# A fifth tile between the halves of the fourth, a one-tile unit's weight splits outside its branch, and a quarter of the descriptor memory

## The chip, the core and the metric

One core of a Trainium2 chip. The metric is the device time of one execution in microseconds. The core has five engines that run queues of instructions of their own and wait for each other by semaphores: TensorE (PE, matmuls and transposes; PEld is its weight loading), ScalarE (ACT), VectorE (DVE), GpSimd (Pool) and SyncE (SP, which here only issues transfers).

## The reference

An attention between tokens and a small state gives 4352 rows of 512 values (8 batches of 512 tokens and 32 state rows, eight heads side by side). Then a mixture of experts works on each row with one expert out of eight:

```python
logits = x @ w_gate
e_idx = np.argmax(logits, axis=1)
gate_w = probs[np.arange(N), e_idx]            # softmax of logits
eom = 1.0 / (1.0 + np.exp(-(x @ w_output_gate)))
for e in range(E):
    mask = e_idx == e
    h = np.maximum(x[mask] @ w1[e], 0.0)       # 512 -> 1024
    ye = h @ w2[e]                             # 1024 -> 512
    out[mask] = gate_w[mask, None] * eom[mask, e, None] * ye
```

## The kernel before

Until about 125 us the kernel does the attention and finds each row's expert. The rest, which the change touches, works through **units**: a unit is up to 512 rows of one expert, with a fifth tile of up to 128 more where the expert's last rows would otherwise need a unit of their own. The counts per expert are 1568, 632, 512, 541, 513, 40, 0 and 546, so nine units are executed, 0 to 8, of 14 in the program; the others lie behind branches. Units 0, 1 and 4 have four full tiles of 128 rows; 2, 3, 5, 6 and 8 have a fifth tile, which is narrow (64 rows or fewer) in four of them; unit 7 holds the 40 rows of expert 5, a single tile. A new expert begins at units 3 to 8.

All matmuls are made of three products: each operand is split into a high half (fp32r) and a low half, `xhi`, `xlo`, `whi`, `wlo`, `hhi`, `hlo`, and hi·hi, hi·lo and lo·hi are added in PSUM. For a unit:

- Pool gathers the unit's rows by indirect transfers, one for each tile (`fetch`, two units ahead), PE transposes them (`transposes`), ACT casts the high half and DVE subtracts for the low one (`x_halves`).
- `blocks` is the first layer, eight blocks f of 128 hidden columns, each with a relu (ACT) and a subtraction (DVE). Which columns stream through PE depends on the unit's class: `cls` 0 is the one-tile unit with a form of its own (rows as the stationary side, two matmul groups into `pbs`, relu into `hs`, eight transposes); 2 is four tiles, 3, 4 and 5 have a fifth.
- `tile_of(t)` is the second layer for a tile: `second` does 24 matmuls 128x512 into `po`, ACT scales the rows by `fac` into `y`, and Pool writes them out by an indirect transfer. `second_narrow` does a narrow fifth tile in 15 matmuls, with an evacuation of three steps (ACT, DVE, ACT).
- Where the next unit has another expert (`chgs`), its weights are split by `halves(i, h)`: for each of four stages i (0 and 1 the first layer's, 2 and 3 the second's) two halves h, each one ACT cast to `whi` and one DVE subtraction to `wlo`. SP loads the stages for a later expert with `load_behind` once they are split.

ACT, DVE, PE and Pool run in the order in which the code is written. Runtime classes are tested by branches on each engine; work in a branch that isn't taken is jumped over. `middle`, called in the middle of tile 0's 24 matmuls, holds splits and transposes for the next unit. Where a branch with transfers isn't taken, Pool executes an INC_SWDGE_SEM, which brings the semaphores of indirect transfers to the value that the others wait for.

Of the kernel before, what the change touches and what calls it, by code (L numbers as in the profile page):

```python
# [14 lines left out]
ALU = mybir.AluOpType  # L15
# [6 lines left out]
def attention_then_top1_experts(ctx: ExitStack, tc: tile.TileContext, x, state, w_gate, w_og, w1, w2, out):  # L22
# [113 lines left out]
    def unit_table():  # L136
# [64 lines left out]
        nc.vector.tensor_tensor(route_i[:, 4, 1:], uf[:, 0, 1:], uf[:, 0, :NU], op=ALU.is_gt)  # L201
        nc.vector.tensor_copy(units_i, cf[:, 5, E - 1 : E])

    tid_sb = const.tile([P, NQ], F32, name="tid_sb")
# [550 lines left out]

    def second(po, hhi, hlo, t, between=None):
        c = slice(P * t, P * t + P)
        for k in range(KH):
            if k == KH // 2 and between is not None:
                between()  # L760
            i, q = 2 + k // 4, k % 4
            nc.tensor.matmul(po, lhsT=hhi[:, k, c], rhs=whi[i][:, q, :], start=(k == 0), stop=False)  # L762
            nc.tensor.matmul(po, lhsT=hhi[:, k, c], rhs=wlo[i][:, q, :], start=False, stop=False)  # L763
            nc.tensor.matmul(po, lhsT=hlo[:, k, c], rhs=whi[i][:, q, :], start=False, stop=(k == KH - 1))  # L764

    def second_narrow(po):

# [30 lines left out]
        nc.scalar.copy(whi[i][:, c, :], stage[i][:, c, :])  # L798
        nc.vector.tensor_sub(wlo[i][:, c, :], stage[i][:, c, :], whi[i][:, c, :].bitcast(F32))  # L799

    def new_halves(i, h, chg):
        with tc.If(of(chg, ET.Activation, ET.DVE) == 1):
            halves(i, h)

    def load_behind(i, chg, s):

        nxt = value(3, s, [ET.SP], E - 1)
        nc.sync.dma_start(stage[i], (w1v if i < 2 else w2v)[bass.ds(nxt, 1), i % 2].rearrange("o p k f -> p (o k) f"),
                          cond=(of(chg, ET.SP) == 1), cond_hint=False)

    for i in (2, 3):
        stage[i] = bp1.tile([P, 4, 512], F32, name=f"stage{i}")
# [10 lines left out]
    hlo = bp1.tile([P, KH, UT * P], F32R, name="hlo")  # L823
    hs = bp1.tile([P, 2, 512], F32, name="hs")

    got, chgs, clss = {}, {}, {}
    table = unit_table()

    def second_stream(b, f, cls):
# [10 lines left out]
    def blocks_of_first_unit(cls, xg):  # L840
        evs = of(cls, ET.Activation, ET.DVE)
        cls = of(cls, ET.PE)
        for f in range(KH):
            if f == 0:
                first(pas[0], f, xhi, xlo, slice(0, NX))

                x_transposed(xg, 2, xhi, xlo)
                x_transposed(xg, 3, xhi, xlo)
            if f + 1 < KH:
                first(pas[(f + 1) % 2], f + 1, xhi, xlo, slice(0, NX))  # L850
            if f == 0:
                x_transposed(xg, 4, xhi, xlo)
            relu(hhi[:, f, :NX], hlo[:, f, :NX], pas[f % 2])
            next(table, None)
            b = pbs[f % 2]
            with tc.If(cls == 2) as c2:
                first(b[:, :256], f, xhi, xlo, slice(NX, NX + 256))
            with c2.Else():
                with tc.If(cls > 2):
                    second_stream(b, f, cls)  # L860
            with tc.If(evs > 2) as c3:
                relu_of_tail(f, b, evs)
            with c3.Else():
# [12 lines left out]
        chgs[1] = value(4, 1, [ET.Activation, ET.DVE, ET.SP], 1)  # L876
        for i in range(4):
            first_weights(i)
        return factors(0, xg)

    def blocks(s, cls, next_rows):

        cls = of(cls, ET.PE, ET.Activation, ET.DVE)
        nxt = chgs.get(s + 1)
        with tc.If(cls == 0) as c0:

            for i in range(2):
                for k in range(KX):
                    for x, w in ((xhi, whi), (xlo, whi), (xhi, wlo)):
                        nc.tensor.matmul(pbs[i], lhsT=x[:, k, :P], rhs=w[i][:, k, :], start=(k == 0 and w is whi and x is xhi),  # L890
                                         stop=(k == KX - 1 and w is wlo))
            new_halves(2, 0, chgs[s])
            new_halves(2, 1, chgs[s])
            nc.scalar.activation(hs[:, 0, :], pbs[0], AF.Relu)
            new_halves(3, 0, chgs[s])
            nc.scalar.activation(hs[:, 1, :], pbs[1], AF.Relu)
            for i, tp in enumerate((pos[1], pbs[0])):
                tp = tp.rearrange("p (q t) -> p q t", t=P)
                c = slice(4 * i, 4 * i + 4)
                for q in range(4):  # L900
                    nc.tensor.transpose(tp[:, q, :], hs[:, i, P * q : P * q + P], ident)
                if i == 0 and nxt is not None:
                    transposes(got[s + 1][1], 0)
# [28 lines left out]
        if nxt is not None:  # L932
            load_behind(0, nxt, s + 1)

    def step(s):
        idt, xg = got[s]
# [8 lines left out]
        if s == 0:  # L945
            fac = blocks_of_first_unit(cls, xg)
        else:
            if s + 2 < NU:
                got[s + 2] = fetch(s + 2)
            fac = factors(s, xg)  # L950
            if more:
                chgs[s + 1] = value(4, s + 1, [ET.Activation, ET.DVE, ET.SP], 1)
            blocks(s, cls, next_rows)
# [10 lines left out]
        def tile_of(t):  # L964
            po, y = pos[t % 2], ys[t % 3]

            def rows_of_tile():
                second(po, hhi, hlo, t, middle if more and t == 0 else None)
                if t == 0 and s and more:
                    next_rows(4)  # L970
# [15 lines left out]
            else:  # L986
                with tc.If(at == 5) as c5:  # L987
                    rows_of_tile()
                with c5.Else():
                    rows_of_narrow_tile()  # L990

        few = of(at, ET.PE, ET.Activation, ET.Pool)
        if s:
            tile_of(0)
            with tc.If(at > 0):
                tile_of(1)
                with tc.If(at > 1):
                    tile_of(2)
                    tile_of(3)
                    with tc.If(at > 2):  # L1000
                        tile_of(4)
        else:
            for t in range(UT):
                if t < 2:
                    for h in range(2):
                        new_halves(t, h, chgs[1])
                    load_behind(t, chgs[1], 1)
                if t == 0:
                    tile_of(0)
                else:  # L1010
                    with tc.If((few if t < UT - 1 else at) > (0, 0, 1, 1, 2)[t]):
                        tile_of(t)
                next_rows(*((), (0, 1), (2, 3), (4,), ())[t])

    with tc.manual_schedule(engines={ET.PE, ET.Activation, ET.DVE, ET.Pool}):
        got[0] = fetch(0)
# [12 lines left out]
        ids(nc.gpsimd, idx, hs[:, :, :NQ], tid_sb)  # L1029
        for s in range(SURE):  # L1030
            step(s)
        units = nc.values_load(units_i, engines=[ET.PE, ET.Activation, ET.DVE, ET.Pool, ET.SP], min_val=SURE, max_val=NU,
                               skip_runtime_bounds_check_because="a sum of rounded-up counts over the experts")
        with ExitStack() as ifs:  # L1034
            for s in range(SURE, NU):
                ifs.enter_context(tc.If(units > s))
                step(s)


# [22 lines left out]
```

## Time and profile before

| | us |
|---|---|
| median of 3 runs (581.37 to 582.8) | 582.47 |
| profiled execution, its own time | 583.2 |
| its span, first to last instruction | 581.1 |
| PE busy | 541.5 |
| DVE, ACT, Pool busy | 258.6, 237.7, 171.0 |

A span is one execution as the hardware profiler saw it. PE is the engine with the most work by far, so time is found where PE waits, and after its last matmul. The durations of single instructions are from this execution. PE's matmuls overlap: one of 128x512 is shown with 0.39 us, but the next begins 0.23 us behind it.

### The profile page before, as it was taken

How to read it: one execution, taken by the hardware profiler on the slowest of the kernel's cores; microseconds unless marked ns; L12 is line 12 of the kernel's file. 1: busy time of each engine (PE TensorE's matmuls, PEld its weight loads, DVE VectorE, ACT ScalarE, POOL GpSimd, SP SyncE). 2: the span in 40 equal slices, each digit the busy share in tenths (PEclk: the TensorE clock that was granted, in tenths of full speed). 3: DMA queues.
4: the chain of work that ended last, by engine and by line, in shares of the span. 5: the costliest groups of instructions: out<-in, count | busy, mean ns of one | idle time of the engine just before them, and what ended most of it. 6: DMA issues, size and time to landing. Idle time of an engine off the chain costs nothing. (4 is left out here: it accounts for less than half of the span.)

```text
span 581.1 us, 11555 instructions
## 1 busy us (share of the span) xinstructions
PE 541.5 (93%) x4028; PEld 462.5 (80%) x4028; DVE 258.6 (44%) x609; ACT 237.7 (41%) x400; POOL 171.0 (29%) x189
## 2 busy tenths in 40 slices
PE   7699989999999999999999999999999999599980
PEld 4578878659987888988998888889889987489860
DVE  3678788646712221360365046226506621755200
ACT  3767867533421221351353144235415423644210
POOL 5117778771534013101500240140024013240110
PEclk9999999999999999999999999999999999799995
DMA  9767524444763002232318133531813451852210
GB/s 252 205 216 234 159 82 147 132 129 150 263 251 118 18 22 83 69 96 105 108 32 295 55 116 103 211 108 50 301 56 105 137 192 48 294 188 76 109 58 12
DMA packets 45047, 78.23 MB, mean 135 GB/s; under 512 B 10312, under 2 KB 18504, under 8 KB 44936
## 3 DMA queue, kind: packets, MB, share of 16 engines
q1 hardware_dynamic: 37624, 52.49, 27.5%
q0 software_dynamic: 7312, 24.31, 12.7%
q8 instruction: 63, 1.03, 0.7%
q14 instruction: 48, 0.39, 0.2%
HBM read 68.38 MB, written 18.90 MB: 150 GB/s over the span
## 5 line engine op out<-in xcount | busy, mean ns | idle before, releaser
L762 PE MATMUL po<-whi,hhi 128*128 128x512 f32 x272 | 109.0, 401 | 4.7 <-ACT whi L798 4.7
L972 POOL DMA_INDIRECT out_dram<-y,idt x30 | 29.4, 981 | 279.4 <-ACT y L971 232.9
L764 PE MATMUL po<-whi,hlo 128*128 128x512 f32 x272 | 107.0, 393 | 0.0
L763 PE MATMUL po<-wlo,hhi 128*128 128x512 f32 x272 | 106.8, 393 | 0.0
L752 PE MATMUL pb<-xhi,whi 128*128 128x288 f32 (+4 forms) x256 | 83.2, 325 | 0.8 <-ACT y L971 0.8
L753 PE MATMUL pb<-xlo,whi 128*128 128x288 f32 (+4 forms) x256 | 83.1, 325 | 0.0
L754 PE MATMUL pb<-xhi,wlo 128*128 128x288 f32 (+4 forms) x256 | 83.1, 325 | 0.0
L971 ACT ACTIVATE y<-po,fac 128x512 f32<-128x512 f32 x34 | 23.5, 690 | 117.7 <-PE po L764 66.9
L799 DVE TENSOR_TENSOR wlo<-stage,whi 128x1024 fp32r<-128x1024 f32 x52 | 63.5, 1224 | 10.7 <-ACT whi L798 8.2
L714 POOL DMA_INDIRECT xg<-xa,idt x50 | 53.7, 1074 | 35.4 <-DVE idt L709 14.9
L762 PEld LDWEIGHTS po<-whi,hhi 128*128 128x128 f32 x272 | 51.6, 190 | 14.9 <-ACT whi L798 4.9
L764 PEld LDWEIGHTS po<-whi,hlo 128*128 128x128 f32 x272 | 51.5, 189 | 11.0
L763 PEld LDWEIGHTS po<-wlo,hhi 128*128 128x128 f32 x272 | 51.7, 190 | 10.1
L752 PE MATMUL pa<-xhi,whi 128*128 128x256 f32 x192 | 54.2, 282 | 3.5 <-ACTq L1000 2.1
L741 DVE TENSOR_TENSOR xlo<-pxT,xhi 128x512 fp32r<-128x512 f32 x50 | 32.7, 686 | 49.9 <-ACT xhi L740 38.3
L753 PE MATMUL pa<-xlo,whi 128*128 128x256 f32 x192 | 53.4, 278 | 1.1 <-issue 0.7
L798 ACT CAST whi<-stage 128x1024 fp32r<-128x1024 f32 x52 | 54.2, 1049 | 0.4 <-ACT ex L726 0.4
L754 PE MATMUL pa<-xhi,wlo 128*128 128x256 f32 x192 | 53.3, 278 | 0.0
L752 PEld LDWEIGHTS pb<-xhi,whi 128*128 128x128 f32 x256 | 48.1, 188 | 4.1 <-issue 1.3
L754 PEld LDWEIGHTS pb<-xhi,wlo 128*128 128x128 f32 x256 | 48.1, 188 | 2.9
L753 PEld LDWEIGHTS pb<-xlo,whi 128*128 128x128 f32 x256 | 48.1, 188 | 2.8
L740 ACT CAST xhi<-pxT 128x512 fp32r<-128x512 f32 x50 | 27.4, 589 | 38.8 <-PE pxT L736 38.2
(228 smaller groups left out, 860.8 us busy)
## 6 DMA issues: line engine op xcount, KB each, us to landing
stage<-in_moe_w_dram SPq DMA_DIRECT2D x42, 1024.0 KB
xa<-xm SPq DMA_DIRECT2D x7, 1056.0 KB
xb<-in_x_dram SPq DMA_DIRECT2D x7, 1024.0 KB
xb<-in_x_dram SPq DMA_DIRECT2D x4, 256.0 KB
xg<-xa,idt POOLq DMA_INDIRECT x50
out_dram<-y,idt POOLq DMA_INDIRECT x34
xa<-xm SPq DMA_DIRECT2D x1, 528.0 KB
sraw<-in_state_dram SPq DMA_DIRECT2D x1, 512.0 KB
```

Of the source, the lines that this page charges most:

```text
L714: nc.gpsimd.indirect_dma_start(out=xg[:, t, :], out_offset=None, in_=xa[:, :], in_offset=bass.IndirectOffsetOnAxis(ap=idt[:, t : t + 1], a ...
L740: nc.scalar.copy(xhi[:, :, c], pxTs[t % 2])
L741: nc.vector.tensor_sub(xlo[:, :, c], pxTs[t % 2], xhi[:, :, c].bitcast(F32))
L752: nc.tensor.matmul(ps, lhsT=hi, rhs=xhi[:, k, cols], start=(k == 0), stop=False)
L753: nc.tensor.matmul(ps, lhsT=hi, rhs=xlo[:, k, cols], start=False, stop=False)
L754: nc.tensor.matmul(ps, lhsT=lo, rhs=xhi[:, k, cols], start=False, stop=(k == KX - 1))
L762: nc.tensor.matmul(po, lhsT=hhi[:, k, c], rhs=whi[i][:, q, :], start=(k == 0), stop=False)
L763: nc.tensor.matmul(po, lhsT=hhi[:, k, c], rhs=wlo[i][:, q, :], start=False, stop=False)
L764: nc.tensor.matmul(po, lhsT=hlo[:, k, c], rhs=whi[i][:, q, :], start=False, stop=(k == KH - 1))
L798: nc.scalar.copy(whi[i][:, c, :], stage[i][:, c, :])
L799: nc.vector.tensor_sub(wlo[i][:, c, :], stage[i][:, c, :], whi[i][:, c, :].bitcast(F32))
L972: nc.gpsimd.indirect_dma_start(out=out[:, :], out_offset=bass.IndirectOffsetOnAxis(ap=idt[:, t : t + 1], axis=0), in_=y, in_offset=None)
```

## The change

1. **Tile 4** (`last_tile`) is called between the halves of tile 3's 24 matmuls instead of behind them. `second` does its products in pairs of k.
2. **The one-tile unit's splits.** Row 4 of `route_i`, which told whether the expert changes (1), tells 2 if the unit has at most 128 rows. In the branch `cls == 0` only the split of (2, 0) stays; (2, 1), (3, 0) and (3, 1) follow behind the branch, in an `If` of their own that other units pass by. The next unit's transposes and `x_halves` of tiles 0 and 1 are arranged around them.
3. **The next unit's first-layer weights** (stages 0 and 1, four halves) are split behind tile 0, with `next_rows(3, 4)`; before, stage 0 was split in `blocks` and stage 1 in `middle`, which now holds only the transposes of tile 2. `fac` is worked out behind `blocks`.
4. **`dynamic_dma_scratch_size`**, the memory for the descriptors of Pool's indirect transfers, is 4096 where the default was 16384 (bytes for each partition).

```diff
-    def new_halves(i, h, chg):
-        with tc.If(of(chg, ET.Activation, ET.DVE) == 1):
+    def new_halves(i, h, chg, small=False):
+        chg = of(chg, ET.Activation, ET.DVE)
+        with tc.If(chg == 2 if small else chg > 0):
             halves(i, h)
...
+            nc.scalar.activation(hs[:, 0, :], pbs[0], AF.Relu)
             new_halves(2, 0, chgs[s])
-            new_halves(2, 1, chgs[s])
-            nc.scalar.activation(hs[:, 0, :], pbs[0], AF.Relu)
-            new_halves(3, 0, chgs[s])
             nc.scalar.activation(hs[:, 1, :], pbs[1], AF.Relu)
...
-            new_halves(3, 1, chgs[s])
-            if nxt is not None:
-                x_halves(0, xhi, xlo)
-                next_rows(1)
-                for h in range(2):
-                    new_halves(0, h, nxt)
...
-                elif f in (5, 6) and nxt is not None:
-                    new_halves(0, f - 5, nxt)
             if nxt is not None:
-                next_rows(0, 1)
+                transposes(got[s + 1][1], 0)
+                transposes(got[s + 1][1], 1)
+
+        new_halves(2, 1, chgs[s], True)
+        if nxt is not None:
+            x_halves(0, xhi, xlo)
+        new_halves(3, 0, chgs[s], True)
+        new_halves(3, 1, chgs[s], True)
+        if nxt is not None:
+            x_halves(1, xhi, xlo)
...
             if s:
-                new_halves(1, 0, chgs[s + 1])
-                next_rows(2, 3)
-                new_halves(1, 1, chgs[s + 1])
-                load_behind(1, chgs[s + 1], s + 1)
+                next_rows(2)
...
+        def last_tile():
+            with tc.If(at > 2):
+                tile_of(4)
...
-            tile_of(0)
+            tile_of(0, middle if more else None)
+            if more:
+                next_rows(3, 4)
+                for i in range(2):
+                    for h in range(2):
+                        new_halves(i, h, chgs[s + 1])
+                    load_behind(i, chgs[s + 1], s + 1)
             with tc.If(at > 0):
                 tile_of(1)
                 with tc.If(at > 1):
                     tile_of(2)
-                    tile_of(3)
-                    with tc.If(at > 2):
-                        tile_of(4)
+                    tile_of(3, last_tile)
...
-    nc = _bacc.Bacc("TRN2", target_bir_lowering=False, num_devices=1)
+    nc = _bacc.Bacc("TRN2", target_bir_lowering=False, num_devices=1, dynamic_dma_scratch_size=4096)
```

ACT in the one-tile unit, before: the stretch of its branch from the two casts of stage 2 (`whi_1979`) to those of stage 0 for the next unit (`whi_109`); the branches skip a cast where the expert doesn't change.

```order
L798 CAST whi_1979<-stage_1978 128x1024
L802 UNCONDITIONAL_BRANCH x2
L802 COMPARE_AND_BRANCH
L798 CAST whi_1979<-stage_1978 128x1024
L802 UNCONDITIONAL_BRANCH x2
L894 ACTIVATE hs<-pb_1958 128x512
L802 COMPARE_AND_BRANCH
L798 CAST whi_1982<-stage_1981 128x1024
L802 UNCONDITIONAL_BRANCH x2
L896 ACTIVATE hs<-pb_1959 128x512
L904 CAST hhi<-po_1961 128x4x128
L904 CAST hhi<-pb_1958 128x4x128
```

The same branch after the change, whole:

```order
L895 COMPARE_AND_BRANCH
L902 ACTIVATE hs<-pb_1958 128x512
L812 COMPARE_AND_BRANCH
L807 CAST whi_1979<-stage_1978 128x1024
L812 UNCONDITIONAL_BRANCH x2
L904 ACTIVATE hs<-pb_1959 128x512
L912 CAST hhi<-po_1961 128x4x128
L912 CAST hhi<-pb_1958 128x4x128
L895 UNCONDITIONAL_BRANCH
```

The first relu stands ahead of all casts, one cast stands between the relus, and the other three have left the branch.

ACT behind `middle` of tile 0, before: the rest of stage 1's split for the next unit (`whi_111`), the last transposed tile and tile 0's evacuation.

```order
L740 CAST xhi<-pxT_1954 128x4x128
L740 CAST xhi<-pxT_1955 128x4x128
L802 COMPARE_AND_BRANCH
L798 CAST whi_111<-stage_108 128x1024
L802 UNCONDITIONAL_BRANCH x2
L740 CAST xhi<-pxT_1954 128x4x128
L971 ACTIVATE y_1975<-po_1960,fac_1974 128x512
L995 COMPARE_AND_BRANCH
```

After, from the transposed tile 2 on (the cast of `whi_111` stands twice behind these rows in the same way, ahead of the branch of tile 1):

```order
L742 CAST xhi<-pxT_1954 128x4x128
L976 ACTIVATE y_1975<-po_1960,fac_1974 128x512
L742 CAST xhi<-pxT_1955 128x4x128
L742 CAST xhi<-pxT_1954 128x4x128
L812 COMPARE_AND_BRANCH
L807 CAST whi_109<-stage_107 128x1024
L812 UNCONDITIONAL_BRANCH x2
L812 COMPARE_AND_BRANCH
L807 CAST whi_109<-stage_107 128x1024
L812 UNCONDITIONAL_BRANCH x2
```

Tile 0's evacuation moves ahead of two transposed tiles, and all four casts of the next unit's first-layer weights come behind it.

Pool at a unit's end, before: the output transfer of tile 3, the branch of tile 4 with its two forms, and the semaphore instruction (ISA) for the case that it isn't taken.

```order
L972 DMA out_dram<-y_1975,idt_1963 4480x512
L1000 COMPARE_AND_BRANCH
L987 COMPARE_AND_BRANCH
L972 DMA out_dram<-y_1976,idt_1963 4480x512
L987 UNCONDITIONAL_BRANCH
L981 DMA out_dram<-y_1976,idt_1963 4480x512
L987 UNCONDITIONAL_BRANCH
L1000 ISA
L1000 UNCONDITIONAL_BRANCH
```

And after:

```order
L998 COMPARE_AND_BRANCH
L992 COMPARE_AND_BRANCH
L977 DMA out_dram<-y_1976,idt_1963 4480x512
L992 UNCONDITIONAL_BRANCH
L986 DMA out_dram<-y_1976,idt_1963 4480x512
L992 UNCONDITIONAL_BRANCH
L998 ISA
L998 UNCONDITIONAL_BRANCH
L977 DMA out_dram<-y_1975,idt_1963 4480x512
```

Tile 3's transfer (`y_1975`) has moved behind tile 4's.

## Rows read from the trace of the kernel before

**Rows 1.** The page: busy us of each engine, share, instructions.
```profile
PE 541.5 (93%) x4028; PEld 462.5 (80%) x4028; DVE 258.6 (44%) x609; ACT 237.7 (41%) x400; POOL 171.0 (29%) x189
```

**Rows 2.** Windows: stretch, length, busy us (instructions) by engine, granted clock, DMA share, GB/s.
```profile
core 0: us, PE busy (x) PEld busy (x) DVE busy (x) ACT busy (x) POOL busy (x), PEclk, DMA share, GB/s
500.00:506.25 6.25, 4.16 (x10) 3.32 (x11) 4.56 (x5) 2.42 (x3) 0.00 (x0) 0.50 1.00 354
```

**Rows 3.** Line 802: queue, instruction, durations ns (min/median/max), first and last start.
```profile
L802 PEldq COMPARE_BRANCH  x1: 5563/5563/5563, 496.4 to 496.4; - x1
```

**Rows 4.** Timeline of unit 7: start, us, engine, operation, idle before and releaser.
```profile
493.60 0.40 PE L890 MATMUL pb<-wlo,xhi 128*128 128x512 f32 x1
...
495.69 0.60 ACT L896 ACTIVATE hs<-pb 128x512 f32<-128x512 f32 x1
...
496.34 0.65 PE L901 MATMUL pb<-ident,hs 128*128 128x128 f32 x4 [0.34 <-ACT hs L896]
...
502.09 0.77 PE L762 MATMUL po<-whi,hhi 128*128 128x512 f32 x1 [4.66 <-ACT whi L798]
```

**Rows 5.** Line 1034, PE's queue; the longest is the last executed unit's.
```profile
L1034 PEldq COMPARE_BRANCH  x4: 65/124/3757, 484.9 to 565.3; - x4
```

**Rows 6.** Timeline from the end of tile 0 of unit 7 into unit 8.
```profile
510.27 0.39 PE L764 MATMUL po<-whi,hlo 128*128 128x512 f32 x1
...
511.13 0.58 ACT L740 CAST xhi<-pxT 128x512 fp32r<-128x512 f32 x1 [1.58 <-PE pxT L736]
511.62 0.69 ACT L971 ACTIVATE y<-po,fac 128x512 f32<-128x512 f32 x1
...
513.46 0.30 PE L752 MATMUL pb<-xhi,whi 128*128 128x320 f32 x1
```

**Rows 7.** The page's groups: the two instructions of a split; busy us, mean ns.
```profile
L799 DVE TENSOR_TENSOR wlo<-stage,whi 128x1024 fp32r<-128x1024 f32 x52 | 63.5, 1224 | 10.7 <-ACT whi L798 8.2
...
L798 ACT CAST whi<-stage 128x1024 fp32r<-128x1024 f32 x52 | 54.2, 1049 | 0.4 <-ACT ex L726 0.4
```

**Rows 8.** Timeline of PE at the ends of units 1 and 4.
```profile
225.54 0.39 PE L763 MATMUL po<-wlo,hhi 128*128 128x512 f32 x1
225.76 0.39 PE L764 MATMUL po<-whi,hlo 128*128 128x512 f32 x1
227.24 0.38 PE L752 MATMUL pa<-xhi,whi 128*128 128x256 f32 x1 [1.09 <-ACTq L1000]
...
382.30 0.39 PE L764 MATMUL po<-whi,hlo 128*128 128x512 f32 x1
383.65 0.39 PE L752 MATMUL pa<-xhi,whi 128*128 128x256 f32 x1 [0.96 <-ACTq L1000]
```

**Rows 9.** Pool's semaphore instruction, by lines: durations ns (min/median/max), first and last start.
```profile
L1011 POOLq INC_SWDGE_SEM  x1: 557/557/557, 179.7 to 179.7; - x1
L1000 POOLq INC_SWDGE_SEM  x2: 710/1004/1297, 227.1 to 383.7; - x2
L995 POOLq INC_SWDGE_SEM  x1: 1842/1842/1842, 512.7 to 512.7; - x1
L1034 POOLq INC_SWDGE_SEM  x1: 2027/2027/2027, 570.4 to 570.4; - x1
```

**Rows 10.** Windows, Pool alone: gathers (the first two rows), then outputs.
```profile
0.00:181.00 181.00, 16.36 (x15) 1.00 0.56 180
0.00:570.40 570.40, 58.70 (x55) 0.99 0.42 137
...
0.00:181.00 181.00, 3.93 (x4) 1.00 0.56 180
0.00:570.40 570.40, 36.96 (x38) 0.99 0.42 137
```

**Rows 11.** Line 1058, the program's end.
```profile
L1058 POOLq DRAIN  x3: 46/107/7670, 572.6 to 580.9; - x3
```

**Rows 12.** The chain that ended last, its pieces in order of time: start, us, what.
```profile
562.38 2.76 DMA out_dram<-y,idt
...
567.41 0.90 POOL out_dram L981
```

More of the change, by code (lines that the diff above doesn't have):

```diff
@@ L200, in unit_table @@
         nc.vector.memset(route_i[:, 4, :], 0)
-        nc.vector.tensor_tensor(route_i[:, 4, 1:], uf[:, 0, 1:], uf[:, 0, :NU], op=ALU.is_gt)
+        nc.vector.tensor_tensor(uf[:, 7, 1:], uf[:, 0, 1:], uf[:, 0, :NU], op=ALU.is_gt)
+        nc.vector.tensor_scalar(uf[:, 6, :], uf[:, 5, :], float(P), 1.0, op0=ALU.is_le, op1=ALU.add)
+        nc.vector.tensor_tensor(route_i[:, 4, 1:], uf[:, 7, 1:], uf[:, 6, 1:], op=ALU.mult)
         nc.vector.tensor_copy(units_i, cf[:, 5, E - 1 : E])
@@ L757, in second, with product @@
         c = slice(P * t, P * t + P)
-        for k in range(KH):
+        def product(k, h, w, stop=False):
+            i, q = 2 + k // 4, k % 4
+            nc.tensor.matmul(po, lhsT=h[:, k, c], rhs=w[i][:, q, :], start=(k == 0 and h is hhi and w is whi), stop=stop)
+        for k in range(0, KH, 2):
             if k == KH // 2 and between is not None:
                 between()
[L761 to L764, printed above, removed]
+            for a in range(2):
+                product(k + a, hhi, whi)
+            for a in range(2):
+                product(k + a, hhi, wlo)
+                product(k + a, hlo, whi, stop=(k + a == KH - 1))
     def second_narrow(po):
@@ L808, in load_behind @@
         nc.sync.dma_start(stage[i], (w1v if i < 2 else w2v)[bass.ds(nxt, 1), i % 2].rearrange("o p k f -> p (o k) f"),
-                          cond=(of(chg, ET.SP) == 1), cond_hint=False)
+                          cond=(of(chg, ET.SP) > 0), cond_hint=False)
     for i in (2, 3):
@@ L824, in attention_then_top1_experts @@
     hs = bp1.tile([P, 2, 512], F32, name="hs")
-    got, chgs, clss = {}, {}, {}
+    got, chgs, clss, units = {}, {}, {}, []
     table = unit_table()
@@ L875, in blocks_of_first_unit @@
         got[2] = fetch(2)
-        chgs[1] = value(4, 1, [ET.Activation, ET.DVE, ET.SP], 1)
+        chgs[1] = value(4, 1, [ET.Activation, ET.DVE, ET.SP], 2)
         for i in range(4):
@@ L879, in blocks_of_first_unit, with blocks @@
         return factors(0, xg)
-    def blocks(s, cls, next_rows):
+    def blocks(s, cls):
         cls = of(cls, ET.PE, ET.Activation, ET.DVE)
@@ L901, in blocks @@
                     nc.tensor.transpose(tp[:, q, :], hs[:, i, P * q : P * q + P], ident)
-                if i == 0 and nxt is not None:
-                    transposes(got[s + 1][1], 0)
+                if nxt is not None:
+                    transposes(got[s + 1][1], i)
                 nc.scalar.copy(hhi[:, c, :P], tp)
                 nc.vector.tensor_sub(hlo[:, c, :P], tp, hhi[:, c, :P].bitcast(F32))
-            new_halves(3, 1, chgs[s])
-            if nxt is not None:
-                x_halves(0, xhi, xlo)
-                next_rows(1)
-                for h in range(2):
-                    new_halves(0, h, nxt)
         with c0.Else():
@@ L925, in blocks @@
                     new_halves(2 + f // 2, f % 2, chgs[s])
-                elif f in (5, 6) and nxt is not None:
-                    new_halves(0, f - 5, nxt)
             if nxt is not None:
-                next_rows(0, 1)
+                transposes(got[s + 1][1], 0)
[5 more added lines that the diff above has]
+        new_halves(3, 1, chgs[s], True)
+        if nxt is not None:
+            x_halves(1, xhi, xlo)
         for i in (2, 3):
             load_behind(i, chgs[s], s)
-        if nxt is not None:
-            load_behind(0, nxt, s + 1)
     def step(s):
@@ L949, in step @@
                 got[s + 2] = fetch(s + 2)
+            if more:
+                chgs[s + 1] = value(4, s + 1, [ET.Activation, ET.DVE, ET.SP], 2)
+            blocks(s, cls)
             fac = factors(s, xg)
-            if more:
-                chgs[s + 1] = value(4, s + 1, [ET.Activation, ET.DVE, ET.SP], 1)
-            blocks(s, cls, next_rows)
         def middle():
@@ L958, in middle, with tile_of @@
             if s:
-                new_halves(1, 0, chgs[s + 1])
-                next_rows(2, 3)
-                new_halves(1, 1, chgs[s + 1])
-                load_behind(1, chgs[s + 1], s + 1)
-        def tile_of(t):
+                next_rows(2)
+            if s == SURE - 2:
+                units.append(nc.values_load(units_i, engines=[ET.PE, ET.Activation, ET.DVE, ET.Pool, ET.SP], min_val=SURE, max_val=NU,
+                                            skip_runtime_bounds_check_because="a sum of rounded-up counts over the experts"))
+        def tile_of(t, between=None):
             po, y = pos[t % 2], ys[t % 3]
             def rows_of_tile():
-                second(po, hhi, hlo, t, middle if more and t == 0 else None)
-                if t == 0 and s and more:
-                    next_rows(4)
+                second(po, hhi, hlo, t, between)
                 nc.scalar.activation(y, po, AF.Copy, scale=fac[:, t : t + 1])
@@ L990, in tile_of @@
                     rows_of_narrow_tile()
+        def last_tile():
+            with tc.If(at > 2):
+                tile_of(4)
         few = of(at, ET.PE, ET.Activation, ET.Pool)
         if s:
-            tile_of(0)
+            tile_of(0, middle if more else None)
+            if more:
+                next_rows(3, 4)
[3 more added lines that the diff above has]
+                    load_behind(i, chgs[s + 1], s + 1)
             with tc.If(at > 0):
@@ L998, in step @@
                     tile_of(2)
-                    tile_of(3)
-                    with tc.If(at > 2):
-                        tile_of(4)
+                    tile_of(3, last_tile)
         else:
-            for t in range(UT):
+            for t in range(UT - 1):
                 if t < 2:
@@ L1008, in step @@
                 if t == 0:
-                    tile_of(0)
-                else:
-                    with tc.If((few if t < UT - 1 else at) > (0, 0, 1, 1, 2)[t]):
-                        tile_of(t)
-                next_rows(*((), (0, 1), (2, 3), (4,), ())[t])
+                    tile_of(0, middle)
+                elif t < 3:
+                    with tc.If(few > (0, 0, 1)[t]):
+                        tile_of(t)
+                else:
+                    with tc.If(at > 1):
+                        tile_of(3, last_tile)
+                next_rows(*((), (0, 1), (2, 3), (4,))[t])
     with tc.manual_schedule(engines={ET.PE, ET.Activation, ET.DVE, ET.Pool}):
@@ L1031, in attention_then_top1_experts @@
             step(s)
-        units = nc.values_load(units_i, engines=[ET.PE, ET.Activation, ET.DVE, ET.Pool, ET.SP], min_val=SURE, max_val=NU,
-                               skip_runtime_bounds_check_because="a sum of rounded-up counts over the experts")
         with ExitStack() as ifs:
             for s in range(SURE, NU):
-                ifs.enter_context(tc.If(units > s))
+                ifs.enter_context(tc.If(units[0] > s))
                 step(s)
```

## The prediction

> **What bounds the kernel now.** I read the page first: PE is busy for 541.5 of 581.1 us [rows 1], so a gain has to come from the 40 us in which it is not, or from what follows its last matmul. PE's own waits put the largest hole into the one-tile unit: 4.66 us ahead of 502.09, "ACT whi" as releaser [rows 4]. The timeline of the tail shows the other large piece: the last matmul is over at 565.0, the last output transfer starts at 567.41 [rows 12], Pool's INC_SWDGE_SEM follows at 570.4 and its DRAIN from 572.6 [rows 9, 11], and the span ends at 581.1: 16 us without a matmul, over 9.7 of them in these two instructions.
>
> **What the 4.66 us are.** The releaser shown is the last semaphore in the profile, not the thing that ended last. PE's queue holds a COMPARE_BRANCH at 496.4 that took 5.563 us, to 501.9 [rows 3]; the matmul starts 0.13 us behind its end. It is the jump over the ordinary path of `blocks`, which this unit doesn't take. PE's other long jump, over units that aren't executed, took 3.757 us [rows 5], at a time when no weights are loaded. So the stall is not a wait for splits, and splits taken out of the branch can't remove it; they can only let PE come to the jump sooner. The program ahead of the jump is the same length after the change.
> [...]
>
> **One-tile unit and the start of the unit behind it.** Before, hs1's relu starts at 495.69, behind two weight casts, though its block's last matmul (493.60) was over at 494.0 [rows 4]. After, one cast stands between the relus and hs1 is ready at about 494.65; PE reaches the jump at about 494.7 instead of 496.35: 1.6 us sooner. The jump keeps 5.56 us if what slows it is always there, or falls towards 3.76 if the weight loads beside it do (the load of stage 2 now comes only after the jump has begun): 0 to 1.8 us more. Tile 0 has four fewer transposes among its matmuls: 0.5 us.
> On the other side, the four casts of the next unit's first-layer weights now stand behind tile 0. Before, two of them were done while PE stood in the jump, and from the issue of tile 0's last matmul (510.27) to the first pb matmul 3.2 us passed [rows 6]. After, ACT has there y0 (0.69 [rows 6]), two xhi (0.58 each [rows 6]), two casts of 1.05 [rows 7], and DVE's second subtraction, 1.22, ends the chain [rows 7]: 0.39 for the last matmul + 0.69 + 1.16 + 2.10 + 1.22 and some 0.45 for hand-overs, 6.0 us, so 2.8 more. Together 2.8 − 1.6 − 0.5 = **+0.7** with the slow jump and **−1.1** with the fast one. [...] I take **0** between −1.1 and +2.6.
> In the other units these casts fall behind tiles 1 to 4: the four need 4.2 us on ACT and 4.9 on DVE [rows 7], one tile of 24 matmuls at 0.23 lasts 5.5, and the evacuations have that long to spare, so I put them at nothing. Without that cover each of the five changes of expert would cost as much as unit 8's, 2.8.
>
> **Tile 4 between the halves.** At the end of a unit of four tiles PE waits for its own last matmul, goes over the branch of tile 4 and then through the next unit's first branches: 225.76 to 227.24 and 382.30 to 383.65 [rows 8], with 0.23 of it the matmul's pitch, 1.25 and 1.12 us lost. After, the branch lies inside tile 3: the wait for the own matmul (0.39 busy less 0.23) and one branch remain, with no unit's end behind them; I take half, 0.6 each, and the end itself costs nothing. Gain 2.37 − 1.2 = **−1.2**; bounds 0 (the price just moves) and −2.4. The order of products by pairs of k leaves the number of matmuls and costs 0.
> At the end of the kernel the narrow tile's evacuation (three operations, 565.1 to 567.1) would be replaced by one of 0.69, −1.4. But outputs go one after another: the tile-3 transfer issued at 562.38 holds the next for 2.76 [rows 12]. After, tile 4's transfer is ready at about 564.7 (12 matmuls sooner) and lands at 567.45; tile 3's goes then, not at 565.9. That is 567.5 against 567.41: **0**.
>
> **A quarter of the descriptor memory.** INC_SWDGE_SEM took 0.557, 0.710, 1.297, 1.842 and 2.027 us [rows 9]. By the first, 15 + 4 indirect transfers had been issued, by the last 55 + 38 = 93 [rows 10]: (2.027 − 0.557) / 74 = 19.9 ns for each transfer in between, and the values at 227, 384 and 513 us lie on that line. So it walks over something that every transfer leaves behind and that hasn't been full or cleared by the 93rd. DRAIN is 46 or 107 ns where nothing has piled up and 7.670 at the end [rows 11]; over 93 that is 82 ns each. If what piles up is entries of the ring, 16384 bytes hold 93 transfers or more, and 4096 hold at least 23. The nearest row to 23 is the INC at 227 us, by that line after 27: 0.71. With 27 to walk, INC falls from 2.03 to 0.71 and DRAIN from 7.67 to 27 × 0.082 = 2.2: −1.3 − 5.4 = **−6.7**, all on the path that ends last, since nothing runs beside them. Bounds: nothing, if the two count transfers and not the ring, and −7.5 at 23 or fewer. What has to be given back to make room costs Pool something, which is busy for 171 of 581 us [rows 1], so up to the tail it is hidden.
> [...]
>
> **Sum.** 0 − 1.2 + 0 − 6.7 = −7.9 from the profiled 583.2 us (span 581.1 and 2.1 around it): 575.3. The median of the runs is 0.7 below the profiled one, so I forecast **574.6**; its own range, by the one-tile unit's bounds (−1.1, +2.6) and the others, is 572 to 577.5.
>
> **Rivals.**
> *The ring has no part in it* (chance 0.20). For: nothing in the trace names what the 19.9 ns are for; a count of transfers would look alike. Against: a counter needs no walk. Then only −1.2 is left: 581.3, with the one-tile unit's bounds 580 to 583.
> *Slower: the small ring is full at the tail* (0.08). With room for some 23 transfers, each later one must first have entries given back. If that is a walk of 0.7 to 2.0 us ahead of each transfer [rows 9], the two last outputs, which go one after the other, pay it twice: up to +4.0, and if DRAIN doesn't shrink, 582.5 − 1.2 + 4.0 = 585.3. For: the ring will wrap some three times. Against: old transfers have long landed by then. It decides when the last transfers take over 3 us more each than their 0.90 [rows 12] and the DRAIN keeps 7.7.
> *The splits were the wait after all* (0.10). Then PE goes on 4.7 us sooner and 2.8 are given back at unit 8: −1.9 more than forecast with the rest, and with the fast tile 0 up to −3: 571.6 to 572.7. For: the releaser named in [rows 4]. Against: [rows 3].
> The forecast has 0.62.
>
> **Numbers.** A measurement of this kernel can tell about 0.3%, 1.75 us, from no change. Below 580.7 lie the forecast, the third rival and a third of the first: 0.78 faster. Within 0.3%: most of the first, 0.13. Slower: the second rival and the first with unit 8's worst case, 0.09. For the range I go down to 571.5 and up to 582.0, which leaves out the slow rival, the upper part of the first and some of the third.
>
> **What would show it.** The last DRAIN at 2 to 2.5 us and the INC before it at 0.7: ring right; 7.7 and 2.0: first rival. INCs of the earlier units stop growing near 0.7. The long PE branch is still there at 3.8 to 5.6 us, starting near 494.7; a restart by 497 would be the third rival. [...] No hole over 0.5 us at the ends of units 1 and 4, and one of 0.5 to 0.6 inside tile 3. The last output transfer starts within 0.5 us of 2.4 us after the last matmul. [...]

## The result, and the profile after

The changed kernel takes 574.89 us (median of 4 runs, 573.4 to 575.9) where the kernel before took 582.2 beside it: a ratio of 0.9873, 95% interval 0.9848 to 0.9899, so 1.3% faster. The forecast was 574.6. That the total agrees to 0.3 us is luck: two gains were put too small and two losses were put at nothing, as the profile shows. The profiled execution has a span of 574.2 us, 6.9 less than before.

The page's line of busy times, against [rows 1]: PE does the same 4028 matmuls, and its share rises mainly because the span shrinks.

```profile
PE 544.5 (95%) x4028; PEld 464.5 (81%) x4028; DVE 259.1 (45%) x611; ACT 240.5 (42%) x400; POOL 171.3 (30%) x189
```

**The ends of Pool's program**, against [rows 9, 11]: the semaphore instruction by its lines (branch of tile 4; of tile 1, in the one-tile unit; of the units that aren't executed) and the drains, durations in ns as minimum, median and maximum.

```profile
L998 POOLq INC_SWDGE_SEM  x3: 440/538/689, 176.7 to 380.0; - x3
L1010 POOLq INC_SWDGE_SEM  x1: 652/652/652, 507.1 to 507.1; - x1
L1048 POOLq INC_SWDGE_SEM  x1: 382/382/382, 571.3 to 571.3; - x1
L1072 POOLq DRAIN  x3: 46/248/973, 571.8 to 573.9; - x3
```

The INCs no longer grow with the program's age; the last is 0.38 us where it was 2.03, the last long DRAIN 0.97 where it was 7.67. Together that is 8.34 us, more than the whole gain.

**The one-tile unit and unit 8**, against [rows 3, 4, 6]: the timeline, then PE's long branch.

```profile
490.68 0.40 PE L900 MATMUL pb<-wlo,xhi 128*128 128x512 f32 x1
...
491.17 0.60 ACT L904 ACTIVATE hs<-pb 128x512 f32<-128x512 f32 x1 [1.19 <-PE pb L900]
...
496.88 1.19 PE L763 MATMUL po<-whi,hhi 128*128 128x512 f32 x2 [3.96 <-ACT whi L807]
...
505.53 0.39 PE L763 MATMUL po<-whi,hlo 128*128 128x512 f32 x1
...
507.54 3.91 ACT L807 CAST whi<-stage 128x1024 fp32r<-128x1024 f32 x4
...
508.64 2.36 DVE L808 TENSOR_TENSOR wlo<-stage,whi 128x1024 fp32r<-128x1024 f32 x2
...
508.66 0.39 PE L754 MATMUL pa<-xhi,whi 128*128 128x256 f32 x1 [1.86 <-ACT whi L807]
...
509.92 0.58 PE L756 MATMUL pa<-xhi,wlo 128*128 128x256 f32 x1 [0.76 <-DVE wlo L808]
...
512.22 0.47 PE L754 MATMUL pb<-xhi,whi 128*128 128x320 f32 x1
```

```profile
L895 PEldq COMPARE_BRANCH  x1: 4868/4868/4868, 491.8 to 491.8; - x1
```

hs1's relu comes right behind its block, PE is in the jump 1.16 us after the issue of the block's last matmul where it was 2.75 (the jump takes 4.87 and ends 0.17 ahead of 496.88), but the hole is still 3.96 us. At unit 8 PE now waits twice for stage 0's splits, once for the cast and once for the subtraction of the first half. Windows of two us, with PE's busy time and the granted clock:

```profile
core 0: us, PE busy (x), PEclk, DMA share, GB/s
496.00:498.00 2.00, 1.12 (x3) 0.54 0.82 208
498.00:500.00 2.00, 2.00 (x6) 0.50 1.01 334
500.00:502.00 2.00, 2.00 (x6) 0.50 1.02 328
502.00:504.00 2.00, 2.00 (x10) 0.76 0.99 355
508.00:510.00 2.00, 0.58 (x3) 0.95 0.35 131
510.00:512.00 2.00, 2.00 (x9) 0.50 0.00 0
```

In this part of the kernel there are two stretches at a granted clock of 0.50 now, one behind the long hole (496.2 to 502.9) and one at unit 8's start (509.8 to 513.2). Before there was one [rows 2]; its ten matmuls would have taken 2.3 us at the pitch of 0.23, so it cost 1.9.

**The ends of units and of the kernel.** The hole at the end of unit 1 [rows 8] is gone: tile 3's last matmul is that of 225.82, and unit 2's first follows with the usual pitch of 0.23. Tile 4's branch now lies 12 matmuls earlier, in the middle of tile 3. There the pitch is 0.54, so 0.31 us are lost, and the same at 175.37 and 379.27 in units 0 and 4. PE's queue went over the branch at 218.87, while matmuls ran, but the semaphore instruction of the branch that isn't taken comes at 223.1, when the matmul of 222.70 has ended.

```profile
222.70 0.39 PE L763 MATMUL po<-whi,hlo 128*128 128x512 f32 x1
223.24 0.70 PE L763 MATMUL po<-whi,hhi 128*128 128x512 f32 x2
...
225.82 0.39 PE L763 MATMUL po<-whi,hlo 128*128 128x512 f32 x1
226.05 0.28 PE L754 MATMUL pa<-xhi,whi 128*128 128x256 f32 x1
```

```profile
L998 PEldq EVENT_SEMAPHORE  x1: 51/51/51, 223.1 to 223.1; - x1
```

The three branches at the start of the next unit (0.17, 0.34 and 0.21 us in PE's queue), which before stood between 226.3 and the next matmul at 227.24, now come at 223.3 to 224.2, beside the second half's matmuls.

The chain that ended last, against [rows 12]: tile 4's transfer starts at 563.89, takes 3.65 us to land, and tile 3's starts at 568.39, 0.85 later still.

```profile
563.89 3.65 DMA out_dram<-y,idt
...
568.39 0.97 POOL out_dram L977
```

**A ledger.** The table below cuts each profiled execution at the same marks, taken from the timelines: the first matmul of unit 0; the issue of the last first-layer matmul of unit 7; the first matmul of its second layer; the issue of its last; unit 8's first pb matmul; the end of the last matmul; the issue of the last output; the last INC; the end of the span. In us:

| from ... to | before | after | difference |
|---|---|---|---|
| span's start ... unit 0 | 129.31 | 129.11 | -0.20 |
| ... unit 7's first layer done | 364.29 | 361.57 | -2.72 |
| ... its second layer starts | 8.49 | 6.20 | -2.29 |
| ... its last matmul | 8.18 | 8.65 | +0.47 |
| ... unit 8's first pb matmul | 3.19 | 6.69 | +3.50 |
| ... last matmul's end | 51.55 | 52.00 | +0.45 |
| ... last output issued | 2.41 | 4.17 | +1.76 |
| ... last INC | 3.00 | 2.87 | -0.13 |
| ... end | 10.73 | 2.93 | -7.80 |

Not all of the -2.72 is the change's. The profiled execution before has a hole of 0.71 us at 446.76 that no other profiled kernel with tile 4 behind tile 3 shows; the same stretch took 363.3 to 363.6 us in four runs built on the kernel before (ring_alone, half_ring, no_splits_in_unit7, late_loads), so 1.7 to 2.0 more than the 361.57 here.

### The profile page after: what moved, and what is told of

It reads as the page before. It is cut to its first block, busy times and chain, and to the rows that moved or that the text cites. A ratio compares the mean times of both kernels' runs of the same rounds, so it can differ in the third digit from the quotient of the medians.

```text
span 574.2 us, 11590 instructions
## 1 busy us (share of the span) xinstructions
PE 544.5 (95%) x4028; PEld 464.5 (81%) x4028; DVE 259.1 (45%) x611; ACT 240.5 (42%) x400; POOL 171.3 (30%) x189
## 3 DMA queue, kind: packets, MB, share of 16 engines
q8 instruction: 63, 1.03, 0.8%
## 5 line engine op out<-in xcount | busy, mean ns | idle before, releaser
L763 PE MATMUL po<-whi,hhi 128*128 128x512 f32 x272 | 87.5, 403 | 4.4 <-ACT whi L807 4.0
L808 DVE TENSOR_TENSOR wlo<-stage,whi 128x1024 fp32r<-128x1024 f32 x52 | 62.0, 1223 | 13.6 <-ACT whi L807 12.7
L763 PEld LDWEIGHTS po<-whi,hhi 128*128 128x128 f32 x272 | 49.5, 191 | 14.7 <-ACT whi L807 4.2
L807 ACT CAST whi<-stage 128x1024 fp32r<-128x1024 f32 x52 | 52.7, 1055 | 0.0
L791 DVE SCALAR_TENSOR_TENSOR hlo<-pb,hhi 128x512 fp32r<-128x512 f32 (+2 forms) x32 | 18.9, 591 | 57.9 <-ACT hhi L790 43.4
```

The costliest lines, as they stand in the source:

```text
L763: nc.tensor.matmul(po, lhsT=h[:, k, c], rhs=w[i][:, q, :], start=(k == 0 and h is hhi and w is whi), stop=stop)
L791: nc.vector.scalar_tensor_tensor(lo, in0=ps, scalar=0.0, in1=dst.bitcast(F32), op0=ALU.max, op1=ALU.subtract)
```

## The experiments

Four kernels that test the descriptor memory and the splits, then four that test the losses, then three more. Ratios are to the kernel before, run beside them, with a 95% interval; where only one run was made, the trace is what is read.

**ring_alone**: the kernel before with the small descriptor memory.

```diff
-    nc = _bacc.Bacc("TRN2", target_bir_lowering=False, num_devices=1)
+    nc = _bacc.Bacc("TRN2", target_bir_lowering=False, num_devices=1, dynamic_dma_scratch_size=4096)
```

> The kernel before with a quarter of the descriptor memory (4096 instead of 16384 bytes) and nothing else. If INC_SWDGE_SEM and DRAIN walk over ring entries that are not yet given back: the last INC falls from 2.03 to about 0.4 us, the last DRAIN from 7.67 to about 1.0, nothing else in the trace moves, and the time falls by 8.3 us to about 573.9. Rival, the new order of the last transfers and not the ring made them short: INC 2.0, DRAIN 7.7, time 582.2.

574.04 us, ratio 0.9863 (0.9831 to 0.9895). The one number gives the whole gain. The last INC took 0.387 and the DRAIN:

```profile
L1058 POOLq DRAIN  x3: 46/107/973, 570.3 to 571.9; - x3
```

The order of the last transfers, the rival, has no part in it.

**old_ring**: the changed kernel with the default size (the same line, taken back).

> The changed kernel with the default descriptor memory (16384). If the ring is the cause, INC and DRAIN grow again to 2.0 and 7.7 us and the time is 574.9 + 8.3 = 583.2, so that the other parts of the change together lose about 1 us. Rival, the order of transfers is the cause: 574.9.

582.4 us, ratio 1.001 (0.9989 to 1.0031). INC and DRAIN are back, to within a nanosecond:

```profile
L1048 POOLq INC_SWDGE_SEM  x1: 2026/2026/2026, 567.1 to 567.1; - x1
...
L1072 POOLq DRAIN  x3: 46/248/7670, 569.3 to 578.0; - x3
```

So the other three parts of the change, together, are worth nothing that can be measured (between 0.1% faster and 0.3% slower).

**half_ring**: the kernel before with 8192 bytes.

> The kernel before with 8192 bytes. If the two instructions walk over what is still in the ring, the INCs stop growing at about twice the quarter ring's highest value (0.69): near 1.2 to 1.4 us, and the last DRAIN lies between 0.97 and 7.67, at most some 4.6 us (56 transfers by 82 ns). Rival, any ring that wraps is cleared as a whole: DRAIN near 1 us as with the quarter.

576.66 us in one run. The INCs rise as before up to 1.30 at 383 us and then fall to 0.84 and 1.03; the DRAIN is between the two others.

```profile
L1000 POOLq INC_SWDGE_SEM  x2: 710/1004/1297, 226.7 to 383.2; - x2
...
L995 POOLq INC_SWDGE_SEM  x1: 842/842/842, 511.3 to 511.3; - x1
...
L1034 POOLq INC_SWDGE_SEM  x1: 1027/1027/1027, 569.0 to 569.0; - x1
L1058 POOLq DRAIN  x3: 46/107/3587, 570.2 to 574.3; - x3
```

By the prices of the kernel before (19.9 ns for each transfer from 0.557 at 19, and 82 ns) the last INC tells 43 transfers, the DRAIN 44: two instructions with different prices count the same thing. With 4096 they tell 10 and 12, by default 93. A count of all transfers doesn't give that. Nor does a ring that is cleared as a whole: at 383 us the INC tells 56, all that had been issued; at 511, after 83, it tells 33, where a ring cleared behind the 56th would hold 27 at most. What fits these counts is that both walk over what is still in the ring, and that entries are given back in batches; the ring itself is in no trace.

**no_splits_in_unit7**: the kernel before; the one-tile unit leaves out the four splits of its second-layer weights, so its 40 rows are worked out with other weights.

```diff
-            new_halves(2, 0, chgs[s])
-            new_halves(2, 1, chgs[s])
             nc.scalar.activation(hs[:, 0, :], pbs[0], AF.Relu)
-            new_halves(3, 0, chgs[s])
             nc.scalar.activation(hs[:, 1, :], pbs[1], AF.Relu)
...
-            new_halves(3, 1, chgs[s])
```

> The kernel before; the one-tile unit leaves out the four splits of its second-layer weights, so that its rows are worked out with the weights of the expert before. If the 4.66 us are the jump over the other units' path, the long COMPARE_BRANCH stays (4.9 to 5.6 us), begins some 1.7 us sooner, and PE waits 4 to 5 us ahead of the second layer. Rival, the stall is the wait for the splits that the profile names: no PE wait over 1 us there, 4.7 us less.

580.6 us in one run. Without any split to wait for, the hole and the branch stay, and the profile still names a cast as releaser:

```profile
498.71 0.77 PE L762 MATMUL po<-whi,hhi 128*128 128x512 f32 x1 [3.13 <-ACT whi L798]
```

```profile
L802 PEldq COMPARE_BRANCH  x1: 4030/4030/4030, 494.5 to 494.5; - x1
```

The hole is the jump (494.51 to 498.54). That it was 1.5 us shorter here neither theory had foretold (see late_loads).

**stage0_early**: the changed kernel; in a one-tile unit stage 0 is split ahead of tile 0.

```diff
         if nxt is not None:
             x_halves(1, xhi, xlo)
+            with tc.If(of(cls, ET.Activation, ET.DVE) == 0):
+                for h in range(2):
+                    new_halves(0, h, nxt)
...
-                for i in range(2):
-                    for h in range(2):
-                        new_halves(i, h, chgs[s + 1])
-                    load_behind(i, chgs[s + 1], s + 1)
+                with tc.If(of(at, ET.Activation, ET.DVE) > 0):
+                    for h in range(2):
+                        new_halves(0, h, chgs[s + 1])
+                load_behind(0, chgs[s + 1], s + 1)
+                for h in range(2):
+                    new_halves(1, h, chgs[s + 1])
+                load_behind(1, chgs[s + 1], s + 1)
```

> The changed kernel, but in a one-tile unit the two splits of the next unit's stage 0 come behind x_halves(1), ahead of tile 0, where ACT and DVE are free under the long jump; other units keep them behind tile 0. If the place of these splits makes unit 8 start late, PE's two holes there (1.86 and 0.76 us) go, together 2 to 2.6 us, and if no second stretch at granted clock 0.50 follows, 1.9 more: 570.4 to 572.9. Rival, unit 8 waits for its transposed rows, which come behind tile 0 too: the holes stay and the time is 574.9.

573.15 us (572.15 to 574.5), ratio 0.9837 (0.9817 to 0.9858), an interval that overlaps the changed kernel's: by the trace the mechanism holds, the time is a little above the range. From tile 0's last matmul to the first pb matmul 4.44 us passed where it was 6.69, and the clock stays at 1.00 behind it; it is still 1.2 more than before, with holes of 0.88 and 0.33 that now end with branches on ACT and DVE.

```profile
500.00:502.00 2.00, 2.00 (x6) 0.50 1.00 329
502.00:504.00 2.00, 2.00 (x10) 0.79 0.99 290
508.00:510.00 2.00, 1.67 (x13) 1.00 0.66 153
510.00:512.00 2.00, 2.00 (x15) 1.00 0.93 288
```

**tile4_last**: the changed kernel with tile 4 behind tile 3 again.

```diff
-                    tile_of(3, last_tile)
+                    tile_of(3)
+                    last_tile()
```

> The changed kernel with tile 4 behind tile 3 again (the pairs of k stay). If the tile's place is what closed the holes at the ends of units 0, 1 and 4, they come back (pitches near 1.0, 1.5 and 1.35 us, together +2.4 to 2.9), and the last output starts 2.4 us behind the last matmul again instead of 4.2: -1.8. Sum 575.6 to 576.0. Rival, other parts of the change closed the holes: they stay closed and only the tail gains, 573.1.

574.14 us (571.0 to 575.97), ratio 0.9833 (0.9802 to 0.9864), between the two expectations, which lie too close together for runs that spread by 5 us. The trace decides what moved: the hole at the end of unit 1 is back, and the first matmul of unit 0 to the first layer of unit 7 took 364.24 us as before (364.29). The last output starts at 569.10, 2.41 behind the last matmul, as before too.

```profile
227.22 0.39 PE L763 MATMUL po<-whi,hlo 128*128 128x512 f32 x1
228.70 0.38 PE L754 MATMUL pa<-xhi,whi 128*128 128x256 f32 x1 [1.10 <-ACTq L998]
```

So tile 4's place closes the units' holes (0.79, 1.09 and 0.96 us before, 0.15 each after: 2.4) and gives 1.8 back at the end of the kernel. The net of that is too small for these times, whose ratio is no worse than the changed kernel's 0.9873.

**tile4_first**: the changed kernel with tile 4 ahead of tile 3.

```diff
-                    tile_of(3, last_tile)
+                    last_tile()
+                    tile_of(3)
...
-            po, y = pos[t % 2], ys[t % 3]
+            po, y = pos[(0, 1, 0, 0, 1)[t]], ys[(0, 1, 2, 1, 0)[t]]
```

> The changed kernel with tile 4 ahead of tile 3 (tile 4 then uses the other PSUM bank, and the y buffers are dealt out anew). If the tail is late because tile 3's output waits for tile 4's to land, tile 4's is issued 2.7 us sooner and has landed when tile 3's rows are ready: the last output starts about 1.1 us behind the last matmul instead of 4.2, and the time is about 571.9. Rival, the place costs PE a wait at the boundary of two tiles and Pool's way to the transfer is what is long: 574.9 or more.

572.98 us (571.11 to 573.99), ratio 0.9824 (0.9801 to 0.9847). The last output starts 1.05 us behind the last matmul (564.31), as expected:

```profile
561.26 0.90 POOL L986 DMA_INDIRECT out_dram<-y,idt  x1 [4.12 <-ACT y L985]
564.40 0.69 ACT L976 ACTIVATE y<-po,fac 128x512 f32<-128x512 f32 x1 [3.41 <-PEq L1050]
565.36 0.97 POOL L977 DMA_INDIRECT out_dram<-y,idt  x1 [3.20 <-ACT y L976]
```

Part of it is paid for at the boundary of tiles 2 and 3 (two holes like this one, at units 1 and 4):

```profile
220.02 0.39 PE L763 MATMUL po<-whi,hlo 128*128 128x512 f32 x1
220.44 0.69 ACT L976 ACTIVATE y<-po,fac 128x512 f32<-128x512 f32 x1 [4.75 <-PE po L763]
221.18 0.50 PE L763 MATMUL po<-whi,hhi 128*128 128x512 f32 x1 [0.78 <-ACTq L998]
```

The branch's own share is the semaphore instruction behind PE's last matmul, at 220.45. The rest is this kernel's deal of the PSUM banks: with `pos[(0, 1, 0, 0, 1)[t]]` tiles 2 and 3 have the same bank, and where tile 4 isn't executed tile 3 starts when ACT has emptied it of tile 2 (220.44 + 0.69 = 221.13). No run gave the two tiles different banks in this order.

**both_moved**: the edits of stage0_early and tile4_first together.

> The two edits of stage0_early and tile4_first together, as a version that should beat both kernels: if the two losses are separate, 574.9 - 3.0 - 2 to 4.5 = 567.4 to 569.9 us. If they share a wait, less is gained than the sum of the two.

570.27 us (570.07 to 572.1), ratio 0.9792 (0.9775 to 0.9809). That is 2.1% faster than the kernel before and beats the changed one. In ratios the two gains are 0.0036 and 0.0049 from 0.9873, and 0.0081 together; but each interval reaches 0.002 to 0.003 to either side, so these times can't tell whether they add up. What is clear of both intervals is that this kernel is faster than the changed one. The time is 0.4 above the range, since each of the two had been put too high.

**late_loads**: the kernel before, with the loads of stages 2 and 3 held back until tile 0 is done, to see whether a load issued just ahead of the jump is what makes it long.

```diff
-        for i in (2, 3):
-            load_behind(i, chgs[s], s)
...
                     next_rows(4)
+                    for i in (2, 3):
+                        nc.vector.tensor_copy(seen[:, i - 2 : i - 1], stage[i][:, 0, 0:1])
+                        load_behind(i, chgs[s], s)
```

> The kernel before, with the loads of stages 2 and 3 held back until tile 0 is done (DVE reads one column of each stage there, and the loads are issued behind it). In the three runs whose first load was issued 0.4 us ahead of the long jump it took 5.3 to 5.7 us, in the others 3.6 to 4.9. [...]

586.65 us in one run. Unit 8 then has a new hole of 4.02 us, a cost that the expectation left out. The jump took 4.32 us where it was 5.56, so 1.2 less:

```profile
L802 PEldq COMPARE_BRANCH  x1: 4317/4317/4317, 495.5 to 495.5; - x1
```

With a load issued just ahead of the jump it took 5.34, 5.56 and 5.71 us, without one 3.61 to 4.93 in ten kernels. So a load just ahead goes with the part above some 4.9 us; what spreads it between 3.6 and 4.9 stays open.

**tile4_in_tile2**: stage0_early with tile 4 between the halves of tile 2, in a PSUM bank of its own.

```diff
-            po, y = pos[t % 2], ys[t % 3]
+            po, y = pos[t % 2] if t < UT - 1 else pbs[0], ys[t % 3]
...
-                    tile_of(2)
-                    tile_of(3, last_tile)
+                    tile_of(2, last_tile)
+                    tile_of(3)
```

> stage0_early with tile 4 between the halves of tile 2 (in a PSUM bank of its own, pb0). In a tile's middle PE doesn't wait for its own last matmul, so the two holes of 0.78 us that tile 4 ahead of tile 3 left (pitch 1.17) go: -1.9 against both_moved. The outputs of tiles 4, 2 and 3 go one after the other, so the last starts some 1.8 us behind the last matmul where it was 1.05: +0.7. Time 569.1. Rival, the untaken branch costs its wait in tile 2 also: 571.

570.79 us (569.67 to 571.8), ratio 0.9803 (0.9779 to 0.9828), no better than both_moved. The two holes of 0.78 are gone and the last output starts 1.20 us behind the last matmul. That PE doesn't wait for its own matmul in a tile's middle, as the expectation has it, was a misreading: the pitch there is 0.54 (217.93 to 218.47), as in the changed kernel. And unit 8's first pb matmul has a new hole of 1.43 us, in the bank that tile 4 now uses; a dependence on tile 4's branch is a likely cause that no run took apart.

```profile
510.63 0.39 PE L754 MATMUL pb<-xhi,whi 128*128 128x320 f32 x1 [1.43 <-DVEq L1016]
```

**eighth_ring**: tile4_in_tile2 with 2048 bytes.

> tile4_in_tile2 with 2048 bytes of descriptor memory. If the ends walk over what is still in the ring: half the room, the last INC at or below 0.4 and DRAIN at or below 0.97 us (at 14 transfers or fewer left, 1.15 at most), so 0 to -0.6 us. Rival, the ring is now too small and Pool's transfers wait for room: DMA_INDIRECT above 1.5 us in several places, and time lost if one is at the tail.

572.56 us (571.24 to 574.17), ratio 0.9835 (0.9812 to 0.9858): no gain. The longest DMA_INDIRECT took 1.93 us, the same as in tile4_in_tile2, so nothing shows that Pool's transfers waited for room, but what is left at the end is not less:

```profile
L1054 POOLq INC_SWDGE_SEM  x1: 451/451/451, 569.2 to 569.2; - x1
...
L1078 POOLq DRAIN  x3: 107/188/1218, 569.8 to 571.9; - x3
```

That is 14 or 15 transfers by the two prices, against 10 to 12 in the quarter. The DRAIN's price, 0.2 us more, is not the whole 1.8 us between the medians; between the profiled executions, which lie 2.7 apart, 1.0 arose ahead of unit 0 and 1.5 behind unit 8's first pb matmul. Both places have a granted clock of 0.50 in this execution (13.6 to 17.0 and 20.4 to 23.8 us; 511.9 to 515.3) and 1.00 in tile4_in_tile2's, so that part is clock, and no run shows that the ring has to do with it.

## Why the prediction was right, point by point

**Ring: right in mechanism, too small by 1.6 us.** Forecast -6.7, measured -8.34 (ring_alone and old_ring confirm it from both sides). The step that was mis-sized is "with 27 to walk": 27 stood for a full ring, but what the INCs count falls and rises: by the price of 19.9 ns, ring_alone's tell 19, 27, 15, 23 and 10 after 19, 27, 56, 83 and 93 transfers, and the program ends with 10 to 12. The rival of a plain count falls with half_ring; the slow rival, a small ring that blocks the tail, did not come even with an eighth of the memory.

**The jump: right.** The third rival falls with no_splits_in_unit7. PE comes to it 1.6 us sooner, as forecast; it took 4.87 us, inside the bounds 3.76 and 5.56. Only its reason was a guess: a load just ahead goes with the longest jumps (5.34 to 5.71 us), but doesn't account for the spread of the others (3.61 to 4.93).

**Unit 8's start: near in size, by another way, and near its worst.** Forecast 6.0 us from tile 0's last matmul, measured 6.69. The chain that was summed, which "DVE's second subtraction" was to end, was over at 511.00, so 5.5 us behind that matmul. PE had been held until 509.92 by the first subtraction, and the ten matmuls left of its first block took 2.3 us at a granted clock of 0.50, at a pitch of 0.21 from the second on, where the 0.115 of the kernel before, at 1.00, gives 1.2: this set unit 8's first pb matmul. The bound of +2.6 is the +0.7 and 1.9 us for a second stretch at 0.50, what the one of [rows 2] cost; it came, 3.4 us long. The one-tile unit and unit 8 together lost 2.1 us in the profiled execution (-2.29 + 0.47 + 3.50 + 0.45), near the bound of +2.6 rather than the 0 that was taken. In old_ring, the same program but for the ring, the same four terms make 70.14 us against 71.41 before, so -1.3: the jump took 3.61 us there, and behind it the granted clock was 1.00 (496 to 504). Zero was a fair middle of a cost that changes from execution to execution. In the other units, where the four casts were put at nothing, no hole appeared: between unit 0's first matmul and the one-tile unit's last block PE's longest wait is 0.36 us.

**Tile 4: too small in the units, wrong at the end.** Forecast -1.2, measured -2.7 between the two profiled executions, of which 0.7 is the hole at 446.76 that only one of them has. Right in kind: the wait for the own matmul remains. The step that was mis-sized is "I take half, 0.6 each": it is 0.31, since the branches behind the wait are gone over while matmuls of the second half run. The third hole, unit 0's, was left out of the sum (0.79 before, 0.15 after). At the end 0 was forecast and 1.8 lost: "lands at 567.45; tile 3's goes then" took the landing time of another transfer, 2.76 us, where this one took 3.65, and nothing for Pool's way from landing to the next issue, 0.85.

**A part that was not foreseen.** Of the 8.34, 7.80 were gained from the last INC's start to the end. Another DRAIN took 0.25 us where the median was 0.107; ring_alone and tile4_last, which end with tile 4's output, have 2.39 and 2.45 us in that stretch and not 2.93, so ring_alone gains the full 8.34. Why is open.

With the measured terms (-0.2 - 2.7 + 2.1 + 1.8 - 0.1 - 7.8) the ledger gives the 6.9 us between the spans; the forecast's -7.9 came close to it by errors of both signs. The ring's part was foreseen; that the others nearly cancel was not.

## What to carry to other kernels

An instruction at the end of a program whose duration grows with the number of transfers before it is worth a look: plot it against that number, and ask which buffer the growth lives in. When the profile names a semaphore as releaser and the producer had finished long before, look at the engine's queue for a branch; a kernel that leaves the suspected work out can settle it in one run. Before a hole is put down to a branch, look at which buffers the work on both sides of it shares. A piece of work that is moved out of the shadow of one stall must be followed to its new place: splits taken out from under the jump became a wait of the next unit, and an output moved ahead of another delayed that one.

## What the runs showed of the hardware that was not expected

- With 16384 bytes the last INC_SWDGE_SEM took 2.03 us behind 93 indirect transfers and the DRAIN 7.67: 19.9 ns more for each transfer behind the 19th, and 82 ns for each of the 93. By these two prices the number counted at the end was 43 or 44 with 8192 bytes, 10 to 12 with 4096, 14 or 15 with 2048 (another order of the outputs): less memory did not always leave less.
- The same long branch of PE took 3.6 to 5.7 us in thirteen kernels, the longest three (5.34, 5.56 and 5.71) where a weight load was issued just ahead of it. What PE waits for in it, no run shows.
- A hole of 3.96 us in PE's work was followed by a stretch at 0.50 of the clock, one of 2.70 (old_ring, the same place) was not, one of 2.82 (stage0_early) was; the two of 1.86 and 0.76 us at unit 8, 1.3 apart, were.
- Tile 4's branch, not taken, cost PE 0.31 us in the middle of tile 3 (changed kernel): its semaphore instruction came at 223.1, when the matmul of 222.70 had ended, and the pitch was 0.54 us instead of 0.23. At the end of a unit, with three more branches behind it, the pitch was 1.48 (225.76 to 227.24, before).
